# Attention in one-bank steps between the products of a mixture, with TensorE's order written out

## The chip, the cores and the metric

One NeuronCore of a Trainium2 chip runs the whole program. The metric is the device time of one execution in microseconds, the median of several runs. The engines are TensorE (PE in the profile, its weight loads PEld), VectorE (DVE), ScalarE (ACT), GpSimd (POOL) and SyncE (SP, which here only issues transfers).

## What is computed

```
# 4 batches, 8 heads, 576 positions, 64 per head; x is [2304, 512]
scores = q @ k.T / 8;  masked: heads 0-3 the last 32 positions, heads 4-7 every 32nd before
x  = softmax(scores) @ v            # heads side by side
x  = (x @ w_a) * (x @ w_b) @ w_out  # first mixture, 512 -> 1536 -> 512, weights float64
logits = x @ w_gate + log1p(exp(x @ w_noise)) * noise
# the two best of 8 experts per token, weights by softmax over the two
out[token] += weight * relu(x @ w1[e]) @ w2[e]   # 512 -> 1024 -> 512
```

## The kernel before

**Stages.** The first mixture runs in five chunks c of tokens: 512 of each of the four batches, and the four rests of 64 as a fifth of 256. A chunk has twelve steps f of 128 hidden columns. `stage_a` makes `pa` and `pb` (four blocks of 128 of the model width, each three products of a high and a low part, `mm3`, lines 184 to 186), copies `pa` to `a` (line 583), multiplies by `pb` (line 590) and splits the result into `gh` and `gl`. `stage_b` adds the step's share to four outputs `po`, one mixture step later (`prev`). Then eight experts follow.

**Attention.** Batch 0 comes first (`us`), batch 1 beside chunk 0, batches 2 and 3 beside chunks 1 and 2. A `Unit` is a pair of heads; `HPS` orders the four units of a batch, two local and two strided. `T` transposes q and k (line 244), `Q` makes masked scores (274), `E` the softmax (293 to 308; "wide" units with one subtraction, one exponential and one sum, others with an exponential for each block, line 303), `P` transposes the weights (317), copies them (318) and multiplies by v (328). Each is a generator that yields after one or more PSUM banks. Outside batch 0 all of it works in two banks with the tag `t`, which `finish` uses too.

**Queues.** `attq` holds the attention of the next batch, `bgq` the background: `finish` (transposes a chunk's output, line 384, multiplies by the router's weights, 393, and scatters token numbers into a table, `route`), `load_expert` (weights of an expert, lines 141 to 145), `fetch` (gathers tokens of an expert, 639, and transposes them, 648). `point`, three times a mixture step, takes some turns of each queue, so the program's text interleaves them; but the order on each engine is that of a scheduler which estimates times and takes what it thinks ready.

**Weights.** The first mixture's float64 weights come in blocks (`load_m1`), are converted by `split64` (lines 165 to 174, six VectorE and two ScalarE instructions a block) and stand in three units of four steps. The third unit, for f=8 to 11, has no room before batch 1's attention has ended (`drain(); conv_to(30); a1.close()` at f=6 of chunk 0). `late_setup` loads the router's constants and writes the zeros of `out` after the last block.

Of the kernel before, what the change touches and what calls it, by code (L numbers as in the profile page):

```python
# [32 lines left out]
def attention_moe_kernel(ctx: ExitStack, tc: tile.TileContext, q, k, v, w_a, w_b, w_out,  # L33
# [26 lines left out]
    maskS = cpool.tile([72, 4, 72], BF, name="maskS")  # L60
# [10 lines left out]
    with tc.tile_pool(name="setup", bufs=1) as sp:  # L71
# [16 lines left out]
        for i in range(4):  # L88
            nc.vector.tensor_add(maskS[:, i, :], r3f[:, 0], r3f[:, 1])
# [16 lines left out]
    def late_setup():  # L106
        nc.sync.dma_start(wg[:, :, 0:8], w_gate.rearrange("(k p) e -> p k e", p=128))
        nc.sync.dma_start(wg[:, :, 8:16], w_noise.rearrange("(k p) e -> p k e", p=128))
        for b in range(B):
# [11 lines left out]
        zero = rpool.tile([128, DM], F32, name="zero", tag="row", bufs=4)  # L121
        nc.vector.memset(zero, 0.0)
        nr = (NT + PAD) // 128
        nc.sync.dma_start(out.rearrange("(p r) d -> p r d", p=128),
                          zero[:, None, :].to_broadcast([128, nr, DM]))
# [24 lines left out]
    def load_raw(src, m):  # L150

        raw = conv_room["raw"](m)
        last_load[0] = nc.sync.dma_start(raw.rearrange("p (n m) c -> p n (m c)", n=src.shape[1]), src)
        return raw

    last_load = [None]

    def split64(raw, hi, lo):
# [3 lines left out]
        ct = conv_room["ct"](raw.shape[1])  # L162
        m, t = ct[:, 0, :], ct[:, 1, :]
# [3 lines left out]

        nc.vector.tensor_scalar(t, Hw, 0x1FF, None, op0=OP.bitwise_and)
        nc.vector.scalar_tensor_tensor(L.bitcast(F32), L.bitcast(U32), 2.0 ** -32, t, op0=OP.mult, op1=OP.add)
        yield  # L170
        nc.vector.scalar_tensor_tensor(m, Hw, i32(0x80000000), m, op0=OP.bitwise_and, op1=OP.bitwise_or)
        nc.scalar.activation(hi, v(m.bitcast(F32)), AF.Copy)  # L172
        nc.vector.tensor_scalar(Hw, m, i32(0xFF800000), None, op0=OP.bitwise_and)
# [23 lines left out]
    class Unit:  # L197
# [36 lines left out]
        def T(self):  # L234


            n, g = self.n, self.g
            self.qT, self.kT = (self.tile(t, [128, S]) for t in ("qT", "kT"))
            for src, dst, act in ((self.ql, self.qT, True), (self.kl, self.kT, False)):
                dv = dst.rearrange("c (p j) -> c j p", j=6) if self.local else dst.rearrange("c (j p) -> c j p", j=8)  # L240
                for half in range(2):
                    ps = self.bank("T", [128, g, n])
                    for jj in range(g):
                        nc.tensor.transpose(ps[:, jj, :], src[:, g * half + jj, :, :], ident[:n, :n])
                    if act:
                        nc.scalar.activation(dv[:, g * half:g * half + g, :], ps, AF.Copy)
                    else:
                        nc.vector.tensor_copy(dv[:, g * half:g * half + g, :], ps)  # L248
                    yield
# [5 lines left out]
        def Q(self, half):  # L255
            n, g, m = self.n, self.g, self.m
            msk = maskAB[:, half:half + 3, :] if self.local else maskS
            s = self.s[half] = self.tile("s", [n, 2, g, m])
            st = self.tile("sst", [96, 1 if self.wide else 2, 8])
            self.mx, self.sm[half] = st[:n, 0, 0:2 * g], st[:n, 0 if self.wide else 1, 0:2 * g]  # L260
            self.src = []
            for x in range(2):
                ps = self.bank("Q", [n, g, m])
                if self.pemask:
                    nc.tensor.matmul(ps, identb[:n, :n], msk, start=True, stop=False)
                for ii in range(g):
                    hh, jl = self.group(x, ii)
                    i = g * half + jl
                    if self.local:
                        r0, q0, k0 = 64 * hh, 96 * i, 96 * i - 32 if i else 0  # L270
                    else:
# [645 lines left out]
```

## Time and profile before

| | |
|---|---|
| median of 3 runs | 1211.13 us (1207.8 to 1213.44) |
| the profiled execution | 1204.69 us, its span 1202.9 us |
| TensorE busy | 1132.1 us, 94% |
| VectorE, ScalarE, GpSimd busy | 540.9, 404.7, 146.2 us |
| mean granted clock | 0.95 of full speed |

The rows come from the profiled execution, whose own time is 6.4 us under the median. [...] A busy time sums the durations of instructions that may overlap, so it bounds work from above.

### The profile page before, as it was taken

How to read it: one execution, taken by the hardware profiler on the slowest of the kernel's cores; microseconds unless marked ns; L12 is line 12 of the kernel's file. 1: busy time of each engine (PE TensorE's matmuls, PEld its weight loads, DVE VectorE, ACT ScalarE, POOL GpSimd, SP SyncE). 2: the span in 40 equal slices, each digit the busy share in tenths (PEclk: the TensorE clock that was granted, in tenths of full speed). 3: DMA queues.
4: the chain of work that ended last, by engine and by line, in shares of the span. 5: the costliest groups of instructions: out<-in, count | busy, mean ns of one | idle time of the engine just before them, and what ended most of it. 6: DMA issues, size and time to landing. Idle time of an engine off the chain costs nothing.

```text
span 1202.9 us, 16056 instructions
## 1 busy us (share of the span) xinstructions
PE 1132.1 (94%) x6381; PEld 953.0 (79%) x6381; DVE 540.9 (45%) x1154; ACT 404.7 (34%) x866; POOL 146.2 (12%) x136
## 2 busy tenths in 40 slices
PE   6989987899998999989999979999999999999996
PEld 4767765687876778878889869988899998898995
DVE  7899346825256524361313734235433434332111
ACT  4555444422133313241213533235333333232111
POOL 0000000000002000200200122222112222221012
PEclk9979967999996899978999989999999999999998
DMA  7653013590012100030000562337526454433033
GB/s 189 168 170 126 15 29 105 148 335 18 20 50 62 36 20 11 23 108 5 1 1 36 146 151 57 78 79 214 155 79 149 105 125 114 123 93 58 5 40 47
DMA packets 89430, 105.03 MB, mean 87 GB/s; under 512 B 43520, under 2 KB 50304, under 8 KB 89344
## 3 DMA queue, kind: packets, MB, share of 16 engines
q1 hardware_dynamic: 79232, 82.89, 23.6%
q0 software_dynamic: 10112, 21.02, 9.3%
q8 instruction: 52, 0.85, 0.3%
q14 instruction: 34, 0.28, 0.1%
HBM read 78.53 MB, written 25.35 MB: 86 GB/s over the span
## 4 chain that ended last, share of the span: by engine, by line
PE 66%; DMA 8%; DVE 4%; ACT 3%; issue 2%; POOL 1%; SPq 0%; ACTq 0%; DVEq 0%; POOLq 0%
PE ph L184 5%; PE ph L185 5%; PE py L184 5%; PE ph L186 5%; DMA st<-in_moe_w_dram 5%; PE py L185 5%; PE py L186 5%; PE pa L184 3%; PE pa L185 3%; PE pa L186 3%; PE po L184 3%; PE po L185 3%; PE pb L186 3%; PE pb L185 3%; PE pb L184 3%; PE po L186 3%
## 5 line engine op out<-in xcount | busy, mean ns | idle before, releaser
L767 DVE SCALAR_TENSOR_TENSOR hl<-ph,hh 128x256 fp32r<-128x256 f32 (+1 forms) x128 | 62.1, 489 | 195.3 <-ACT hh L766 191.5
L766 ACT ACTIVATE hh<-ph 128x256 fp32r<-128x256 f32 (+1 forms) x128 | 55.1, 434 | 206.4 <-PE ph L186 204.0
L463 POOL DMA_INDIRECT table<-pay,sli x36 | 38.0, 1056 | 669.2 <-DVE sli L450 650.3
L590 DVE TENSOR_TENSOR a<-a,pb 128x512 f32<-128x512 f32 (+1 forms) x60 | 37.9, 631 | 124.9 <-PE pb L186 119.1
L791 POOL DMA_INDIRECT out_dram<-y,tb x40 | 64.7, 1618 | 189.1 <-ACT y L790 126.6
L583 ACT ACTIVATE a<-pa 128x512 f32<-128x512 f32 (+1 forms) x60 | 33.2, 553 | 115.9 <-PE pa L186 109.6
L591 ACT ACTIVATE gh<-a 128x512 fp32r<-128x512 f32 (+1 forms) x60 | 35.2, 587 | 107.0 <-DVE a L590 92.9
L639 POOL DMA_INDIRECT g<-x,tb x40 | 40.9, 1022 | 190.7 <-PE tt L648 161.7
L318 ACT ACTIVATE pT<-tt 128x288 f32<-128x288 f32 (+1 forms) x64 | 25.4, 408 | 73.9 <-PE tt L317 69.0
L592 DVE TENSOR_TENSOR gl<-a,gh 128x512 fp32r<-128x512 f32 (+1 forms) x60 | 38.1, 636 | 23.2 <-ACT gh L591 23.2
L328 PE MATMUL tt<-pT,vl 72*64 72x72 f32 (+1 forms) x448 | 40.0, 306 | 3.2 <-ACT pT L318 2.4
L274 PE MATMUL tt<-kT,qT 64*72 64x72 f32 (+1 forms) x336 | 39.0, 290 | 3.5 <-DVE kT L248 2.0
L274 PEld LDWEIGHTS tt<-kT,qT 64*72 64x72 f32 (+1 forms) x336 | 31.5, 178 | 13.2 <-issue 5.6
L184 PE MATMUL pa<-xh,w6h 128*128 128x512 f32 (+1 forms) x80 | 31.8, 398 | 10.5 <-ACT w6h L172 6.5
L328 PEld LDWEIGHTS tt<-pT,vl 72*64 72x64 f32 (+1 forms) x448 | 28.7, 181 | 16.2 <-ACT pT L318 8.6
L317 PE MATMUL tt<-ident,s 72*72 72x72 f32 (+1 forms) x224 | 34.0, 299 | 4.4 <-DVE s L308 2.1
L184 PE MATMUL pa<-xh,w0h 128*128 128x512 f32 (+1 forms) x80 | 34.7, 434 | 1.9 <-ACT xh L366 1.6
L317 PEld LDWEIGHTS tt<-ident,s 72*72 72x72 f32 (+1 forms) x224 | 26.0, 164 | 13.0 <-issue 4.1
L185 PE MATMUL pa<-xl,w0h 128*128 128x512 f32 (+1 forms) x80 | 33.9, 423 | 2.4 <-DVE xl L367 2.4
L184 PE MATMUL py<-w6h,hh 128*128 128x512 f32 x80 | 31.9, 400 | 4.4 <-ACT y L790 2.5
L184 PE MATMUL py<-w2h,hh 128*128 128x512 f32 x80 | 32.6, 408 | 2.1 <-ACT hh L766 1.3
L186 PE MATMUL pa<-xh,w0l 128*128 128x512 f32 (+1 forms) x80 | 32.4, 405 | 0.0
(292 smaller groups left out, 3296.2 us busy)
## 6 DMA issues: line engine op xcount, KB each, us to landing
st<-in_moe_w_dram SPq DMA_DIRECT2D x64, 512.0 KB
out_dram<-zero SPq DMA_DIRECT2D x1, 6656.0 KB
x<-row SPq DMA_DIRECT2D x16, 256.0 KB
raw<-in_moe_w_a_dram SPq DMA_DIRECT2D x6, 512.0 KB
raw<-in_moe_w_b_dram SPq DMA_DIRECT2D x6, 512.0 KB
raw<-in_moe_w_out_dram SPq DMA_DIRECT2D x6, 512.0 KB
raw<-in_moe_w_a_dram SPq DMA_DIRECT2D x3, 1024.0 KB
raw<-in_moe_w_b_dram SPq DMA_DIRECT2D x3, 1024.0 KB
```

Of the source, the lines that this page charges most:

```text
L184: nc.tensor.matmul(ps, w[0], x[0], start=start, stop=False)
L185: nc.tensor.matmul(ps, w[0], x[1], start=False, stop=False)
L186: nc.tensor.matmul(ps, w[1], x[0], start=False, stop=stop)
L274: nc.tensor.matmul(ps[:, ii, :], self.qT[r0:r0 + 64, q0:q0 + n], self.kT[r0:r0 + 64, k0:k0 + m], start=not self.pemask, stop=not self.pema ...
L317: nc.tensor.transpose(ps[:, ii, :], self.s[half][:, x, ii, :], ident[:n, :n])
L328: nc.tensor.matmul(ps[64 * hh:64 * hh + 64, jl, :], self.vl[:, hh, g * half + jl, :], pT[:, x, ii, :], start=True, stop=True)
L463: ins = nc.gpsimd.indirect_dma_start(out=table, out_offset=bass.IndirectOffsetOnAxis(ap=sli[:, 2 * j + kk:2 * j + kk + 1], axis=0), in_=pa ...
L592: nc.vector.tensor_sub(gl, a, gh.bitcast(F32))
L639: nc.gpsimd.indirect_dma_start(out=g, out_offset=None, in_=x2, in_offset=bass.IndirectOffsetOnAxis(ap=TB[e, t][:, 0:1], axis=0))
L766: nc.scalar.activation(hh, ph, AF.Relu)
L767: nc.vector.scalar_tensor_tensor(hl, ph, 0.0, hh.bitcast(F32), op0=OP.max, op1=OP.subtract)
L791: ins = nc.gpsimd.indirect_dma_start(out=out, out_offset=bass.IndirectOffsetOnAxis(ap=TB[e, t][:, 0:1], axis=0), in_=y, in_offset=None, co ...
```

## The change

Attention's generators become plain functions that each fill one bank (`T(i)`, `Q(half, x)`, `P(half, x)`, `PV(half)`, with `E` called at the end of the second `Q`), and `att_pipe` writes out their order with a yield after each. The loop over mixture steps stands in a block that keeps TensorE's instructions in the order of the program (`manual_schedule`). `point` comes six times a step, every six products, and takes one attention step; `bgq` gets a turn at each third point, in the last chunk at each second. The buffers of the conversion leave the attention pool, so the weights of f=8 and 9 get room right after batch 0, and those of f=10 and 11 take over the conversion's own buffers. Batch 0 uses no wide units. `split64` needs one scratch row of a block in place of two; the strided mask is kept once and broadcast; rows of the chunk's output are held in pairs. The zeros of `out` are written in 13 parts in the background of chunk 3 (`clear_out`), the router's constants loaded at the start of chunk 1.

```diff
+    def clear_out():
+        zero = xpool["g"].tile([128, DM], F32, name="zero", tag="x00h")
         nc.vector.memset(zero, 0.0)
         nr = (NT + PAD) // 128
...
         nc.sync.dma_start(x2[NT:NT + PAD, :].rearrange("(p r) d -> p r d", p=128),
                           zero[:, None, :].to_broadcast([128, PAD // 128, DM]))
+        yield
         for b in range(B):
             nc.sync.dma_start(x2[S * b + CT:S * b + S, :], zero[:TL, :])
+        yield
+        to = out.rearrange("(p r) d -> p r d", p=128)
+        for r in range(0, nr, 2):
+            nc.sync.dma_start(to[:, r:r + 2, :], zero[:, None, :].to_broadcast([128, 2, DM]))
+            yield
...
+            if self.wide and i // 2:
+                nc.vector.tensor_copy(dv[:, g * half:g * half + g, :], ps)
+            else:
+                nc.scalar.activation(dv[:, g * half:g * half + g, :], ps, AF.Copy)
...
+            if x == 1:
+                self.E(half)
...
+    def att_pipe(us, ahead, done=None):
+        for i in range(4):
+            us[0].T(i)
+            yield
+        if ahead < len(us):
+            us[ahead].load_qk()
+        if ahead == 2:
+            us[1].load_v()
+        for n, u in enumerate(us):
+            last = us[n - 1] if n else None
+            nxt = us[n + 1] if n + 1 < len(us) else None
+            for x in range(2):
+                u.Q(0, x)
+                yield
+            if last:
+                for x in range(2):
+                    last.P(1, x)
+                    yield
+            u.Q(1, 0)
+            yield
+            if last:
+                last.PV(1)
+                if done:
+                    done(last)
+                if n + ahead - 1 < len(us):
+                    us[n + ahead - 1].load_v()
+                yield
+            u.Q(1, 1)
+            yield
+            for i in range(2):
+                if nxt:
+                    nxt.T(i)
+                    yield
+            for x in range(2):
+                u.P(0, x)
+                yield
+            for i in range(2, 4):
+                if nxt:
+                    nxt.T(i)
+                    yield
+            if nxt and n + 1 + ahead < len(us):
+                us[n + 1 + ahead].load_qk()
+            u.PV(0)
+            yield
+        for x in range(2):
+            u.P(1, x)
+            yield
+        u.PV(1)
+        if done:
+            done(u)
+        yield
...
+    def last_units(pool, f, tags):
+        three = []
+        for i in range(3):
+            shape = [128, 2, KD, 256] if i < 2 else [128, 2, 2, 512]
+            w = pool.tile(shape, F32R, name=f"w{f}{i}", tag=tags[i])
+            three.append((w[:, 0], w[:, 1]))
+        for i in range(2):
+            W[f + i] = (*three, i)
...
-        for f, n in [(0, 1), (1, 1), (2, 2), (4, 2), (6, 2)] + [(f, 1) for f in range(8, NF)]:
+        for f, n in [(0, 1), (1, 1), (2, 2), (4, 2), (6, 2), (8, 2), (10, 1), (11, 1)]:
...
-    us = [Unit(p1tile, bank0, 0, hp, True, i % 2 == 1) for i, hp in enumerate(HPS)]
+    us = [Unit(p1tile, bank0, 0, hp, True, False) for hp in HPS]
...
+    a1.close()
+    tp = m1.enter_context(tc.tile_pool(name="third", bufs=1, reuse_waits="tile"))
+    att = ExitStack()
+    apool = att.enter_context(tc.tile_pool(name="att", bufs=1, side="right", reuse_waits="tile"))
+    last_units(tp, 8, ("w80", "w81", "w82"))
+    def atile(name, shape):
+        if name in ("ql", "kl"):
+            return stage.tile(shape, F32, name=name, tag=f"st{int(name == 'kl')}")
+        return apool.tile(shape, F32, name=name, tag=name, bufs=2 if name in ("s", "sst") else 1)
+    def attend(b, wide):
+        us = [Unit(atile, bank1, b, hp, False, wide) for hp in HPS]
+        us[0].load_qk()
+        us[0].load_v()
+        return att_pipe(us, 1)
+    attq.append(attend(1, False))
...
+        def half(tag, w):
+            ps = psum.tile([128, n], F32, name="pa" if tag == "A" else "pb", tag=tag)
+            for i, kd in enumerate(HPS):
+                mm3(ps, tuple(t[:, kd, cols] for t in w), xT[c, kd], i == 0, i == KD - 1)
+                if i == 1:
+                    point()
+            return ps
+        pa = half("A", wa)
...
+            if 2 * (j + 1) in (J, 2 * J):
+                point()
...
+    with tc.manual_schedule(engines={mybir.EngineType.PE}):
+        prev = None
+        npt = [0]
+        for c, f in ORDER:
+            n0, n1 = nconv[0], min(48, 12 + 4 * (f + 1) if f < 6 else 36 + 6 * (f - 5))
+            def point():
+                npt[0] += 1
+                if c == 0:
+                    conv_to(n0 + (n1 - n0) * ((npt[0] - 1) % 6 + 1) // 6)
                 advance(attq)
...
+                if npt[0] % (2 if c == NCH - 1 else 3) == 0:
+                    advance(bgq)
+            if c == 0 and f == 6:
+                conv_to(36)
+                last_units(cp, 10, ("u0", "u1", "u2"))
+                conv_room["raw"] = lambda m: rpool.tile([128, 512, 2], I32, name="raw", tag=f"row{next_of(2)}")
+                conv_room["ct"] = lambda m: rpool.tile([128, 512], I32, name="ct", tag="x2T")
+            if f == NF - 1:
+                while attq:
+                    advance(attq)
+                if c == 0:
+                    conv_to(48)
+            if c == 1 and f == 0:
+                late_setup()
+            if (c, f) == (B - 1, 0):
+                bgq.append(clear_out())
+                att.close()
+                xr = ctx.enter_context(tc.tile_pool(name="xr", bufs=1, side="right"))
+                xpool[0, 0] = xr
+                xpool["g"] = xr
+            if (c, f) == (B - 1, 2):
+                for kd in HPS:
+                    xf[B, kd] = mpool.tile([128, TL * B], F32, name="xf", tag="xf", bufs=4)
+                    nc.sync.dma_start(xf[B, kd], tails[:, kd, :])
+            if 0 < c < B - 1 and f == 0:
+                attq.append(attend(c + 1, True))
+            if (c, f) == (NCH - 1, 5):
+                bgq.append(load_expert(0))
+            if (c, f) == (NCH - 1, 8):
+                bgq.append(fetch(0, [0, 1, 2]))
+            g = stage_a(c, f, point)
+            if f == NF - 1 and c + 1 < NCH:
+                for kd in HPS:
+                    split_kd(c + 1, kd)
+            if prev is not None:
+                rows = stage_b(*prev, point)
+                if rows is not None:
+                    bgq.append(finish(prev[0], rows))
+            prev = (c, f, g)
+        drain()
+        last_rows = stage_b(*prev, pump)
```

## Rows read from the trace of the kernel before

**Rows 1.** The page, part 1: busy time, share of the span, instructions.

```profile
PE 1132.1 (94%) x6381; PEld 953.0 (79%) x6381; DVE 540.9 (45%) x1154; ACT 404.7 (34%) x866; POOL 146.2 (12%) x136
```

**Rows 2.** Stage view: stretch, length, PE, PEld, DVE, ACT, POOL busy (instructions), clock, transfers, GB/s.

```profile
0.00:81.80 81.80, 66.63 (x387) 49.76 (x388) 70.28 (x160) 44.16 (x111) 2.57 (x20) 0.92 0.67 175
81.80:147.30 65.50, 65.28 (x342) 50.58 (x342) 48.04 (x76) 32.79 (x90) 0.00 (x0) 1.00 0.26 82
147.30:197.50 50.20, 41.65 (x267) 31.47 (x266) 23.32 (x49) 23.41 (x84) 0.00 (x0) 0.66 0.17 46
197.50:242.80 45.30, 37.39 (x147) 27.73 (x146) 37.04 (x70) 18.55 (x32) 0.00 (x0) 0.96 0.54 162
242.80:346.50 103.70, 103.70 (x535) 83.85 (x535) 35.26 (x64) 23.84 (x42) 0.00 (x0) 1.00 0.33 103
346.50:398.10 51.60, 45.27 (x314) 34.99 (x313) 33.93 (x89) 20.81 (x40) 8.57 (x8) 0.71 0.28 69
398.10:505.50 107.40, 107.40 (x602) 86.31 (x602) 45.66 (x108) 28.36 (x49) 8.42 (x8) 1.00 0.08 20
505.50:543.00 37.50, 34.43 (x235) 27.31 (x234) 21.66 (x41) 13.94 (x28) 0.26 (x1) 0.81 0.30 92
543.00:643.60 100.60, 100.60 (x461) 82.78 (x461) 24.31 (x73) 20.17 (x35) 8.01 (x8) 0.97 0.01 1
643.60:715.40 71.80, 61.85 (x432) 56.40 (x430) 36.60 (x105) 31.59 (x65) 11.72 (x11) 0.95 0.43 115
715.40:1202.90 487.50, 467.92 (x2673) 421.81 (x2673) 164.74 (x322) 147.07 (x295) 106.62 (x81) 0.99 0.40 97
```

**Rows 3.** TensorE's instructions in order, chunk 1: start, duration, engine, line, operands, count.

```profile
251.68 0.39 PE L184 MATMUL pa<-xh,w0h 128*128 128x512 f32 x1
...
259.35 0.39 PE L184 MATMUL pa<-xh,w0h 128*128 128x512 f32 x1
```

**Rows 4.** TensorE's instructions in order, pause after chunk 1; in brackets the wait before.

```profile
389.50 0.60 PE L328 MATMUL tt<-pT,vl 72*64 72x72 f32 x12 [0.44 <-ACT pT L318]
391.31 0.67 PE L317 MATMUL tt<-ident,s 72*72 72x72 f32 x8 [1.21 <-DVE s L308]
```

**Rows 5.** TensorE's groups by line, 398.1 to 505.5: operands, count, busy us, mean ns, idle.

```profile
L274 PE MATMUL tt<-kT,qT 64*96 64x128 f32 (+1 forms) x68 | 6.5, 260 | 0.0
...
L393 PE MATMUL tt<-wg,x2T 128*128 128x16 f32 x32 | 4.1, 259 | 0.0
...
L317 PE MATMUL tt<-ident,s 72*72 72x72 f32 (+1 forms) x28 | 3.0, 235 | 0.0
L328 PE MATMUL tt<-pT,vl 128*64 128x96 f32 (+1 forms) x40 | 2.5, 247 | 0.0
L384 PE MATMUL tt<-ident,row 128*128 128x128 f32 x16 | 2.4, 272 | 0.0
L244 PE MATMUL tt<-ident,ql 72*128 72x72 f32 (+1 forms) x14 | 1.8, 245 | 0.0
```

**Rows 6.** The page, part 5: costliest groups of the whole span.

```profile
L318 ACT ACTIVATE pT<-tt 128x288 f32<-128x288 f32 (+1 forms) x64 | 25.4, 408 | 73.9 <-PE tt L317 69.0
...
L274 PE MATMUL tt<-kT,qT 64*72 64x72 f32 (+1 forms) x336 | 39.0, 290 | 3.5 <-DVE kT L248 2.0
```

**Rows 7.** ScalarE's groups by line and shape, 0 to 245.

```profile
L303 ACT ACTIVATE s<-s,sst 72x72 f32<-72x72 f32 x32 | 10.8, 342 | 0.7 <-DVE sst L301 0.7
...
L303 ACT ACTIVATION_READ_ACCUMULATOR s<-s,sst 72x1 f32 x32 | 6.0, 188 | 0.0
```

**Rows 8.** TensorE's instructions in order, beside batch 0's attention.

```profile
41.80 0.63 PE L186 MATMUL pa<-xh,w0l 128*128 128x512 f32 x1
42.23 0.63 PE L185 MATMUL pb<-xl,w1h 128*128 128x512 f32 x1
```

**Rows 9.** GpSimd's instructions in order: the first gather.

```profile
706.23 0.99 POOL L639 DMA_INDIRECT g<-x,tb  x1 [10.05 <-PE pb L186]
```

More of the change, by code (lines that the diff above doesn't have):

```diff
@@ new lines, in Q @@
+            msk = maskAB[:, half:half + 3, :] if self.local else maskS[:, None, :].to_broadcast([72, 4, 72])
+            if x == 0:
+                self.s[half] = self.tile("s", [n, 2, g, m])
+                st = self.tile("sst", [96, 1 if self.wide else 2, 8])
+                self.mx, self.sm[half] = st[:n, 0, 0:2 * g], st[:n, 0 if self.wide else 1, 0:2 * g]
+                self.src = []
+            s = self.s[half]
+            ps = self.bank("Q", [n, g, m])
+            if self.pemask:
+                nc.tensor.matmul(ps, identb[:n, :n], msk, start=True, stop=False)
@@ new lines, in Q @@
+            for ii in range(g):
+                hh, jl = self.group(x, ii)
+                i = g * half + jl
+                if self.local:
+                    r0, q0, k0 = 64 * hh, 96 * i, 96 * i - 32 if i else 0
+                else:
+                    r0, q0 = 64 * (i % 2), 72 * (4 * hh + i // 2)
+                    k0 = q0
+                nc.tensor.matmul(ps[:, ii, :], self.qT[r0:r0 + 64, q0:q0 + n], self.kT[r0:r0 + 64, k0:k0 + m],
+                                 start=not self.pemask, stop=not self.pemask or ii == g - 1)
@@ L506, in attention_moe_kernel @@
     ORDER = [(c, f) for c in range(NCH) for f in range(NF)]
-    WA, WB, WO = [None] * 3, [None] * 3, [None] * 3
+    W = {}
     for u in range(2):
-        WA[u], WB[u], WO[u] = (unit_pair(3 * u + i) for i in range(3))
+        three = [unit_pair(3 * u + i) for i in range(3)]
+        for f in range(4 * u, 4 * u + 4):
+            W[f] = (*three, f % 4)
+    def last_units(pool, f, tags):
[6 more added lines that the diff above has]
+            W[f + i] = (*three, i)
+    NPAIR = 18
     def load_m1():
@@ new lines, in load_m1 @@
+        raws = []
+        for k, (_, f, n, i) in enumerate(blocks):
+            while len(raws) < min(k + 2, len(blocks), 99 if k >= NPAIR else NPAIR):
+                raws.append(load_raw(blocks[len(raws)][0], 512 * blocks[len(raws)][2]))
+            at = W[f][3]
+            yield from split64(raws[k], *(t[:, :, 128 * at:128 * (at + n)] if i < 2 else t[:, at:at + n, :]
+                                          for t in W[f][i]))
+    cp = m1.enter_context(tc.tile_pool(name="conv", bufs=1))
@@ L539, in attention_moe_kernel @@
+    conv_room["ct"] = ct_tile
     conv = load_m1()
@@ L584, in stage_a @@
         point()
-        pb = psum.tile([128, n], F32, name="pb", tag="B")
-        for kd in HPS:
-            mm3(pb, tuple(t[:, kd, w[1]:w[1] + 128] for t in WB[w[0]]), xT[c, kd], kd == HPS[0], kd == HPS[-1])
+        pb = half("B", wb)
         gh = mpool.tile([128, n], F32R, name="gh", tag="gh", bufs=2)
```

254 lines of the change are left out of this document (62 added, 192 removed).

## The prediction

> **What bounds the kernel now.** I read the page first: TensorE is busy 94% of the span, every other engine under half [rows 1]. That share hides the question, because a transposition at half clock counts as busy like a product at full clock; so I cut the span at the copies `a<-pa` of line 583, one per mixture step, and read the stages [rows 2]. The bounds are the copies of f=0 of each chunk (81.8, 242.8, 398.1, 543.0, 643.6), the last copy before a pause and the first after it (147.3 and 197.5; 346.5 for f=11 of chunk 1; 505.5 for f=11 of chunk 2), and the first product of the experts (715.4).
>
> The reader is to see two kinds of stretch. In 242.8 to 346.5 and 398.1 to 505.5 TensorE is never idle, at granted clock 1.00. In 147.3 to 197.5, 346.5 to 398.1 and 505.5 to 543.0 hardly a mixture step ends: attention, left over, runs nearly alone, at a mean clock of 0.66, 0.71 and 0.81, with short idle spells. The waits there are of TensorE for what attention itself has just asked of VectorE and ScalarE (0.44 us for a copy of line 318, 1.21 us for the scaled scores of line 308) [rows 4]: chains of one head pair with no other work between. So before 543 us the kernel is bound by TensorE where mixture and attention mix, and by attention's chain and the lower clock where they don't.
>
> **The cost of dense work.** Between two like products of consecutive mixture steps stand 33 products in 7.67 us, so one 512-column product takes 0.2324 us [rows 3]. A step is 36 of them (24 for `pa` and `pb`, 12 for `po`), 8.37 us, a chunk 100.4 us. From the copy of f=0 to that of f=11 lie 11 steps, 92.0 us; in chunk 2 they took 107.4 us [rows 2], so 15.4 us paid for what attention and `finish` had in there. By lines that was 68 of the score products, 28 of the transpositions of line 317, 40 products of line 328, 28 transpositions of q and k (14 of each), and the whole `finish` of one chunk (16 transpositions, 32 router products) [rows 5]. A batch shows 112 score products (336 over three batches [rows 6]; the code writes 56, so each shows as two), by the code also 112 of line 328 and 56 transpositions of either kind: about half a batch was there. If `finish` took 5 us of the 15.4 (its rows are busy 6.5 us, overlapping), half a batch took 10.4 and a batch some 21; if `finish` cost nothing, 31. The new order cuts attention into 56 groups a batch where that stretch had it in larger ones, so I take 27 us.
>
> **The change, part by part.** *Order of the mixture.* TensorE now takes its instructions in the order of the program, and the program offers an attention step at six points of each mixture step, every six products, 1.39 us apart. 72 points a chunk for 56 steps: all of a batch is issued by f=9, none is left for a pause. Chunk 1 becomes 100.4 + 27 + 6 (`finish`) = 133 us against 155.3 now; chunk 2 also 133 against 144.9: -22 and -12.
>
> *Chunk 0.* Now 161.0 us, in which the pause also holds back the third weight unit: its room comes free only when attention of batch 1 is done, and 197.5 to 242.8 then runs step by step behind the conversions. The change gives that room right after batch 0's attention. The floor is 100.4 + 27. VectorE was busy 108.4 us in these 161.0 and ScalarE 74.8 [rows 2], so both fit, VectorE at some 80%. Here batch 1's softmax is still eight (six) exponentials one by one, 0.34 us and 0.19 us for the sum each [rows 7]: about 4 us in which the copies of line 318 and others queue on ScalarE. I add 8 us for that and for the first load of batch 1, which waits for a buffer of batch 0: 135 us, -26. Its bounds: 127, nothing exposed, and 161, the conversions as late as now.
>
> *Batch 0's attention.* No products of chunk 0 need run between it any more, units 1 and 3 move their subtraction and sum from VectorE to ScalarE, and kT is copied by ScalarE. [...] TensorE is busy 66.6 of 81.8 us there, VectorE 70.3, ScalarE 44.2 [rows 2]. Fewer products and less VectorE work pull down, the longer softmax chain pulls up. I take 0; bounds -10 and +8.
>
> *One bank per step, two banks `t`.* A step may reuse a bank two points later, some 3 us after it filled it. The copies that empty it take about 0.41 us [rows 6]; the cover is the 12 products between. Where that cover is short, after a `finish` step that takes the other bank, a copy queued behind a longer instruction can still be late; the 6 us for `finish` hold that. Deeper dependences are further apart: five steps or more from the scores to their transposition, some 9 us.
>
> *Mask in one copy, `split64` with a half-size scratch, paired rows, conversion blocks of two units:* the same operations on the same amounts, off TensorE; 0, at most 1 us.
>
> *Chunk 3.* No attention there: 100.6 us now. But part of its f=0 was run ahead, in the pause before; the new order can't. With `finish` it is 100.4 + 6 less what was done by 543; I take 103, +2. The zeros written to `out` move here from the start of chunk 1, where TensorE was never idle beside them; 0.
>
> *Chunk 4 and the start of the experts.* 71.8 us now, of which 61.9 TensorE was busy [rows 2]; the first gather goes out at 706.2 [rows 9]. A chunk of 256 tokens has half-length `pa` and `pb` products and half as many `po`: 50.2 us at full clock, with `finish` 56. Against that stands a detail of the queues: `clear_out` (15 steps) and `finish` (16) share the 24 turns of chunk 3, so seven steps spill over and `finish` of chunk 3 gets to its scatters only at f=7 of chunk 4, with the experts' weights already taking turns. The transpositions of gathered rows are in TensorE's order too, so it stands still if a gather is late. I take 68, -4; bounds 58 and 90.
>
> **Sum.** -26 - 22 - 12 + 2 - 4 = -62. The profiled execution took 1204.7 us (span 1202.9, 1.8 around it), so 1143 on its scale; the median of the runs is 1211.1, 6.4 us more, so 1149. The experts, 487.5 us, keep their code.
>
> **Rivals.** *Chunk 0 doesn't shrink:* conversions, exponentials and copies share two in-order engines, and TensorE, in order, waits for whatever they put late. For it: from 197.5 to 242.8, where only conversions hold the steps up, VectorE is busy 37.0 of 45.3 us. Against: from 81.8 to 147.3 it converted beside attention (48.0 of 65.5 us) and TensorE was busy 65.3 [rows 2]. Time 1149 + 26 = 1175. Chance 0.09.
>
> *The tail takes it back:* the late scatters cost chunk 4 some 20 us instead of giving 4. 1149 + 20, about 1170. Chance 0.06.
>
> *Waits in order, slower than before:* the scheduler's order let TensorE run mixture products while attention waited; the written one doesn't. 168 attention steps and 48 of `finish` stand in it; if each waits 0.29 us the 62 are gone, with 0.5 us, about the shorter of the two waits shown, the time is 1149 + 108 = 1257. For it: those waits exist [rows 4]. Against: they arise where the next step follows at once, and here 1.39 us of products stand between. Chance 0.06, of which 0.05 ends slower. [...]
>
> *The clock falls in the mixed stretches:* many small groups with short gaps. [...] Against: attention stood between products in the dense stretches and the granted clock was 1.00 [rows 2]. Chance 0.03. [...]
>
> *The order isn't the cause:* the pauses are set by loads and remain, no change, 1211. The waits in them are for VectorE and ScalarE, not DMA; chance 0.02.
>
> **How the numbers follow.** The forecast, chance 0.74, is 1149, rounded to 1150; the bounds of its terms are -8 and +15 (chunk 0 from 127 to 150), -18 and +12 (three batches at 21 or 31), -10 and +8 (batch 0), -10 and +22 (the tail). Taken as independent (root of the sum of squares) they give -24 and +30, 1125 to 1179 for the forecast alone. The range runs from 1115, the two largest low bounds and a little of the others, to 1188, which holds the first two rivals. A change of under 0.5%, about 6 us, can't be told from none. Faster: 0.74 + 0.09 + 0.06 + 0.03 = 0.92. Same: 0.02 and 0.01 of the waits, 0.03. Slower 0.05.
>
> **What would show it.** Copies `a<-pa` at an even pace of some 11 us through chunks 0 to 2 and none more than 15 us apart; granted clock 1.00 from f=1 of chunk 0 to the end of chunk 3; no stretch of attention alone; the experts beginning 60 us earlier, and 487 us long as now. Wrong would be: TensorE idle before lines 274 and 317 at every step (order), gaps named `w..h` in chunk 0 (conversions), or the first gather as far behind f=0 of chunk 4 as now, 63 us, or more (tail).

## The result, and the profile after

The changed kernel took 1170.3 us in the median of four runs (1169.4 to 1178.9), the kernel before on the same chip 1212.0 (1207.8 to 1213.4): a ratio of 0.968, 95% interval 0.963 to 0.973. Forecast were 1150. The profiled execution took 1169.4 us with a span of 1167.6; against the 1204.7 of the one before, 35.3 us went, where the sum said 62.

The stage view of the changed kernel, cut as in [rows 2] at the copies `a<-pa` (now line 666) of f=0 of each chunk and at the first product of the experts:

```profile
0.00:87.46 87.46, 61.27 (x369) 44.70 (x370) 63.21 (x141) 53.00 (x180) 2.28 (x19) 0.90 0.61 160
87.46:223.46 136.00, 131.08 (x760) 100.97 (x758) 99.29 (x166) 76.88 (x208) 0.26 (x1) 0.98 0.35 103
223.46:360.77 137.31, 136.59 (x834) 106.93 (x832) 67.46 (x149) 43.78 (x77) 7.93 (x8) 1.00 0.14 37
360.77:496.98 136.21, 136.21 (x828) 106.74 (x827) 67.91 (x150) 43.09 (x76) 7.74 (x8) 1.00 0.30 97
496.98:600.62 103.64, 103.64 (x482) 85.41 (x481) 25.48 (x69) 21.95 (x37) 0.00 (x0) 1.00 0.09 29
600.62:676.60 75.98, 62.59 (x449) 56.51 (x447) 34.47 (x108) 30.00 (x62) 19.04 (x19) 0.96 0.44 108
676.60:1167.60 491.00, 471.41 (x2674) 425.98 (x2672) 167.48 (x327) 149.29 (x300) 106.71 (x81) 0.98 0.40 97
```

| stretch | before | after | difference | forecast |
|---|---|---|---|---|
| to f=0 of chunk 0 (batch 0's attention) | 81.8 | 87.5 | +5.7 | 0 |
| chunk 0 | 161.0 | 136.0 | -25.0 | -26 |
| chunk 1 | 155.3 | 137.3 | -18.0 | -22 |
| chunk 2 | 144.9 | 136.2 | -8.7 | -12 |
| chunk 3 | 100.6 | 103.6 | +3.0 | +2 |
| chunk 4 to the first expert product | 71.8 | 76.0 | +4.2 | -4 |
| experts | 487.5 | 491.0 | +3.5 | 0 |

The pauses are gone: in chunks 1 and 2 the copies stand 8.2 to 13.4 us apart, TensorE idles 0.7 us in the two together, and the granted clock (TensorE's, as a share of full speed) is 1.00, where the last steps of these chunks had been stretches of attention at 0.71 and 0.81 [rows 2]. Three of the prediction's signs were missed: in chunk 0 one copy stands 17.4 us behind the one before (f=1 to f=2, with a wait of 4.1 us for batch 1's scaled scores), over the 15 allowed; the clock is 0.98 there; and the experts begin 38.8 us earlier, not 60. What the sum lacked is shown by three places.

First, the passage between mixture and attention. TensorE's instructions in order, chunk 2 (start, duration, operands):

```profile
382.77 0.39 PE L187 MATMUL pa<-xl,w0h 128*128 128x512 f32 x1
383.00 0.39 PE L188 MATMUL pa<-xh,w0l 128*128 128x512 f32 x1
383.24 0.41 PE L247 MATMUL tt<-ident,kl 72*128 72x72 f32 x4
383.45 0.48 PE L186 MATMUL pa<-xh,w0h 128*128 128x512 f32 x1
383.77 0.39 PE L187 MATMUL pa<-xl,w0h 128*128 128x512 f32 x1
```

Products follow each other in 0.23 us, as in [rows 3]; the one behind a group of attention holds the next up for 0.32 (383.45 to 383.77). So it is behind all 54 groups that stand between products in chunk 2 (0.31 to 0.34, from start to start). That is 0.09 us a group, 5 us for 56 groups. The product ahead of a group of score products or of line 331 is held up as well, 0.32 to 0.33 in all 24 cases, which is another 2 us.

Second, the waits of TensorE until 88 us (line waited for: total, times, longest):

```profile
PE tt L331 <- ACT pT L319: 5.6, 5, 2.2
...
PE tt L247 <- DMA ql<-in_q_dram: 3.8, 1, 3.8
PE tt L318 <- DVE s L310: 3.7, 2, 3.3
PE tt L318 <- ACT xf L334: 3.2, 2, 3.0
```

In the stage of before the like of the first and the last two came to 0.7 us. Batch 0's last products, before and after (the second line is of the changed kernel):

```profile
75.69 1.55 PE L328 MATMUL tt<-pT,vl 72*64 72x72 f32 x16
78.98 1.28 PE L331 MATMUL tt<-pT,vl 72*64 72x72 f32 x16 [0.44 <-ACT pT L319]
```

They began 3.3 us later; behind them stand the 3.8 us for batch 1's first load, ahead of the copy that ends this stage. ScalarE's groups by line up to 82 us show why batch 0 takes longer: 56 exponentials and 56 sums, 29.6 us, where there were 24 of each and four wide ones.

```profile
L306 ACT ACTIVATE s<-sc,sst 72x72 f32<-72x72 f32 (+1 forms) x56 | 18.0, 339 | 3.7 <-PE tt L331 3.6 <-DVE sst L304 0.2
L306 ACT ACTIVATION_READ_ACCUMULATOR s<-sc,sst 72x1 f32 (+1 forms) x56 | 11.6, 208 | 0.0
```

Third, the tail. SP's issues and GpSimd's and TensorE's instructions in order; the gather of the third fence answers to [rows 9]:

```profile
620.20 31.45 SPq L146 DMA_DIRECT2D st<-in_moe_w_dram  x10
655.58 0.34 SPq L716 DMA_DIRECT2D tb<-table  x1
```

```profile
669.95 1.12 PE L731 MATMUL tt<-ident,g 128*128 128x128 f32 x4 [7.41 <-DMA g<-x,tb]
```

```profile
659.46 1.28 POOL L496 DMA_INDIRECT table<-pay,sli  x1 [9.67 <-issue]
661.04 0.97 POOL L496 DMA_INDIRECT table<-pay,sli  x1 [0.30 <-DMA st<-in_moe_w_dram]
662.31 0.98 POOL L722 DMA_INDIRECT g<-x,tb  x1 [0.30 <-issue]
```

The 31.45 us run from the first to the last of ten issues that took 0.37 to 0.38 us each. These weight loads come ahead of the first table on SP, and four of the eight scatters of chunk 3's router, the last at 664.9, behind it, beside the gathers. The first gather goes out 61.7 us behind the copy of f=0 of chunk 4, about the 63 that I named as the sign of trouble in the tail, and TensorE, which has the transposition of gathered rows in its order, stands 7.4 us ahead of `po` products that were ready.

### The profile page after: what moved, and what is told of

It is laid out like the page before. It is cut to its first block, busy times and chain, and to the rows that moved or that the text cites. A ratio compares the mean times of both kernels' runs of the same rounds, so it can differ in the third digit from the quotient of the medians.

```text
span 1167.6 us, 16084 instructions
## 1 busy us (share of the span) xinstructions
PE 1102.8 (94%) x6381; PEld 927.2 (79%) x6381; DVE 525.3 (45%) x1109; ACT 418.0 (36%) x936; POOL 144.0 (12%) x136
## 4 chain that ended last, share of the span: by engine, by line
PE 78%; DMA 10%; DVE 7%; issue 2%; POOL 2%; ACT 1%; SPq 1%; DVEq 0%; ACTq 0%; POOLq 0%
PE ph L186 6%; PE ph L187 6%; PE ph L188 6%; PE py L186 6%; PE py L187 6%; PE py L188 5%; PE po L186 4%; PE pb L186 4%; PE pa L186 4%; PE pb L188 4%; PE pb L187 4%; PE po L188 4%; PE po L187 4%; PE pa L187 4%; PE pa L188 4%; DMA st<-in_moe_w_dram 3%
## 5 line engine op out<-in xcount | busy, mean ns | idle before, releaser
L672 ACT ACTIVATE gh<-a 128x512 fp32r<-128x512 f32 (+1 forms) x60 | 35.3, 588 | 81.2 <-DVE a L671 80.2
L277 PEld LDWEIGHTS tt<-kT,qT 64*72 64x72 f32 (+1 forms) x336 | 30.4, 149 | 18.2 <-issue 14.9
L318 PE MATMUL tt<-ident,s 72*72 72x72 f32 (+1 forms) x224 | 30.9, 263 | 11.9 <-DVE s L310 7.8
L277 PE MATMUL tt<-kT,qT 64*72 64x72 f32 (+1 forms) x336 | 39.1, 253 | 0.7 <-DVE s L286 0.7
L331 PEld LDWEIGHTS tt<-pT,vl 72*64 72x64 f32 (+1 forms) x448 | 22.3, 156 | 18.6 <-issue 8.6
L331 PE MATMUL tt<-pT,vl 72*64 72x72 f32 (+1 forms) x448 | 29.8, 270 | 5.6 <-ACT pT L319 5.6
L731 PE MATMUL tt<-ident,g 128*128 128x128 f32 x160 | 26.0, 281 | 9.5 <-DMA g<-x,tb 8.1
L731 PEld LDWEIGHTS tt<-ident,g 128*128 128x128 f32 x160 | 20.6, 145 | 15.1 <-DMA g<-x,tb 7.6
L187 PE MATMUL py<-w6l,hh 128*128 128x512 f32 x80 | 32.6, 407 | 0.0
## 6 DMA issues: line engine op xcount, KB each, us to landing
ql<-in_q_dram SPq DMA_DIRECT2D x16, 144.0 KB
```

Source lines behind the costliest of these rows:

```text
L187: nc.tensor.matmul(ps, w[0], x[1], start=False, stop=False)
L277: nc.tensor.matmul(ps[:, ii, :], self.qT[r0:r0 + 64, q0:q0 + n], self.kT[r0:r0 + 64, k0:k0 + m], start=not self.pemask, stop=not self.pema ...
L318: nc.tensor.transpose(ps[:, ii, :], self.s[half][:, x, ii, :], ident[:n, :n])
L331: nc.tensor.matmul(ps[64 * hh:64 * hh + 64, jl, :], self.vl[:, hh, g * half + jl, :], self.pT[:, x, ii, :], start=True, stop=True)
L731: nc.tensor.transpose(ps[:, kd, :], g[:, 128 * kd:128 * kd + 128], ident)
```

## The experiments

Times of whole kernels are medians; stages are read from one profiled execution each. "Before" ran on the same chip each time with medians of 1207 to 1210. The expert stage has the same instructions in all kernels and took 482.6 to 491.0 us in their profiled executions; so differences of a few us are read from the stages ahead of it and not from the totals. Stages have a spread too: up to f=0 of chunk 0 the eight kernels that keep the changed one's batch 0 and its loads took 84.5 to 88.1 us, and the seven that keep its tail took 75.2 to 80.2 us from f=0 of chunk 4 to the first expert product.

**The order without the rest, and the rest without the order.** The first kernel is the changed one with the block around the mixture's loop taken out:

```diff
-    with tc.manual_schedule(engines={mybir.EngineType.PE}):
+    if True:
```

> The changed kernel without the block that fixes TensorE's order: attention's one-bank steps, the earlier weight rooms and all else are kept, and TensorE's instructions are again placed by the scheduler. Theory (the order is the cause): attention is again left over at the ends of chunks 0 to 2, stretches without a mixture step come back, and the time returns to between 1190 and 1215 us. Rival (the small steps and the early rooms are what helps): no such stretch, within 10 us of the changed kernel's 1170.

Measured: 1191.4, ratio 0.984 (0.978 to 0.991). ScalarE's copies `a<-pa` in order, the two around the end of chunk 1, and the stage between them (columns as above):

```profile
338.32 0.60 ACT L666 ACTIVATE a<-pa 128x512 f32<-128x512 f32 x1 [1.25 <-PE pa L188]
...
373.54 0.60 ACT L666 ACTIVATE a<-pa 128x512 f32<-128x512 f32 x1 [2.06 <-PE pa L188]
```

```profile
334.00:373.54 39.54, 32.85 (x251) 25.74 (x250) 20.76 (x43) 14.60 (x29) 8.08 (x8) 0.86 0.28 76
```

The pause is back: 35.2 us without a mixture step, TensorE busy 32.9 of 39.5. Chunks 0 to 2 end with such steps of 39.1, 35.2 and 40.1 us, where before they had one each of 50.2, 51.6 and 37.5. So the theory's sign is there, but not its whole price: of some 40 us, 21 hang on the order (1191.4 less 1170.3), the other 19 came without it, by shorter pauses in chunks 0 and 1 (142.2 and 144.0 us); which of the change's other parts gave them, no run shows.

The second kernel is the one before with only its loop put into such a block (the same line, added there).

> The kernel before, with nothing changed but that its first mixture stands in the block that fixes TensorE's order: attention's steps as before, several of them at each of three points of a mixture step, the third weight unit's room free as late as before. Theory (the order takes the pauses away by itself, but with several groups behind one point it pays waits for banks and for copies, and chunk 0 keeps its late room): no step more than 20 us long in chunks 1 and 2, which take 140 to 150 us each, chunk 0 155 to 165; 1190 to 1205 in all. Rival 1 (the order alone gives the whole gain): 1165 to 1175. Rival 2 (in order, without the small steps, the waits outweigh the pauses): over 1216.

Measured: 1203.7, ratio 0.995 (0.992 to 0.998). Chunk 0 took 152.5, chunk 1 166.0, chunk 2 144.8. SP's issues and TensorE's first step of batch 2, in order:

```profile
222.04 11.58 SPq L126 DMA_DIRECT2D x<-zero  x1
233.66 9.01 SPq L129 DMA_DIRECT2D x<-zero  x4
242.77 3.22 SPq L216 DMA_DIRECT2D ql<-in_q_dram  x2
```

```profile
251.37 1.19 PE L244 MATMUL tt<-ident,ql 96*128 96x96 f32 x6 [20.98 <-DMA ql<-in_q_dram]
```

The pauses are gone, but one step of 36.7 us stands at the start of chunk 1: the issues on zeros hold SP for 20.6 us, batch 2's first load is behind them, and the mixture behind the step that needs it. My expectation of 140 to 150 for chunk 1 missed that; without the 21 us it would have held. Order alone gives 0.5%, the rest alone 1.6%, both 3.2%: the order needs loads that come early enough for it.

**The zeros.** In the changed kernel they were written in one go again at the start of chunk 1:

```diff
 def late_setup():
     ...
+        zero = rpool.tile([128, 2, DM], F32, name="zero", tag="row1")[:, 0]
+        nc.vector.memset(zero, 0.0)
+        nc.sync.dma_start(out.rearrange("(p r) d -> p r d", p=128), ...)
+        nc.sync.dma_start(x2[NT:NT + PAD, :].rearrange("(p r) d -> p r d", p=128), ...)
+        for b in range(B):
+            nc.sync.dma_start(x2[S * b + CT:S * b + S, :], zero[:TL, :])
     ...
-                bgq.append(clear_out())
```

> The changed kernel with the zeros of the output and of the padding rows written in one go at the start of chunk 1, as before, instead of in 15 turns of chunk 3. Theory (SP's queue works in order and its issues stall behind those zeros, so batch 2's first load comes some 20 us late, and in the written order the mixture stands behind the transposition that needs it; with the order alone one such wait took 21.0 us): one step of chunk 1 takes over 28 us, chunk 1 18 to 24 us longer, chunk 3 unchanged, and from the copy of f=0 of chunk 4 to the first expert product 4 to 8 us less than 76.0, since the router gets its turns; 1178 to 1190 in all. Rival (the zeros are hidden wherever they stand, as I priced them): chunk 1 within 2 us, 1160 to 1167.

Measured: 1183.7, ratio 0.980 (0.975 to 0.985). SP's issues, then TensorE's step that needs the load:

```profile
185.84 0.64 SPq L123 DMA_DIRECT2D out_dram<-zero  x1
186.53 11.04 SPq L125 DMA_DIRECT2D x<-zero  x1
197.61 5.66 SPq L128 DMA_DIRECT2D x<-zero  x1
...
204.76 1.23 SPq L242 DMA_DIRECT2D vl<-in_v_dram  x1
```

```profile
213.68 1.23 PE L340 MATMUL tt<-pT,vl 72*64 72x72 f32 x16 [17.70 <-DMA vl<-in_v_dram]
```

The price was right, the place wrong. SP's queue is still placed by the scheduler, which put the zeros ahead of batch 1's last load of v, so one step late in chunk 0 took 31.2 us; the copy of f=0 of chunk 1 came at 244.7 instead of 223.5, chunk 1 took 137.8. The tail went from 76.0 to 69.5, as expected of the turns that became free. So the zeros were no cost only because they moved: left where they were they cost 21 us up to f=0 of chunk 1, and 13 in all. In the kernel before they held SP as long (21.4 us, from 235.4 to 256.8); SP's issues and TensorE's first step of batch 2 there:

```profile
236.12 10.87 SPq L126 DMA_DIRECT2D x<-zero  x1
...
256.92 3.23 SPq L216 DMA_DIRECT2D ql<-in_q_dram  x2
```

```profile
266.35 0.66 PE L244 MATMUL tt<-ident,ql 96*128 96x96 f32 x6
```

That step came 23.5 us into chunk 1, and TensorE ran on with products until then without a pause [rows 2]. In the changed kernel the issues of the zeros stand at the end of chunk 2:

```profile
473.43 0.59 SPq L125 DMA_DIRECT2D x<-zero  x1
...
479.07 17.86 SPq L133 DMA_DIRECT2D out_dram<-zero  x13
```

They still fill 23.5 us of SP, so cutting them into parts didn't make them shorter; they cost nothing because TensorE waits for no load there (it is never idle in chunks 2 and 3).

**How attention is cut.** Two steps at every second point, and six at one point of a mixture step:

```diff
-                advance(attq)
+                if npt[0] % 2 == 0:
+                    advance(attq)
+                    advance(attq)
```

> Attention advances two steps at every second point (behind 12 products) instead of one at every point (behind 6). Theory (what my 27 us for a batch missed is the passage between mixture and a small group: 432 mixture products beside attention took 107 us where they take 100 alone, some 0.12 us for each of 56 groups): half as many passages, chunks 0 to 2 each 3 to 4 us shorter, about 1160 in all. Rival 1 (the cost lies in the groups' own instructions): chunks unchanged within 1 us. Rival 2 (the second group of a pair waits for a bank): some 0.3 us for each of 28 pairs, each chunk 5 to 8 us longer.

Measured: 1166.7, ratio 0.964 (0.958 to 0.969). Chunks 1 and 2 of the pairs:

```profile
224.84:360.41 135.57, 133.71 (x833) 107.48 (x832) 66.65 (x149) 41.70 (x77) 7.94 (x8) 1.00 0.14 37
360.41:495.99 135.58, 133.72 (x831) 107.54 (x830) 67.13 (x150) 41.72 (x78) 7.73 (x8) 1.00 0.30 97
```

TensorE is busy 2.9 and 2.5 us less than in the changed kernel, 0.09 to 0.10 us for each of the 28 passages that the code saves. (In chunk 1's rows the groups between products fall from 56 to 33, since some steps stand beside one of `finish`; that is 0.13 us for each, as the product ahead of some groups gains too.) Waits rise from 0.7 and 0 to 1.9 us a chunk, so 1.7 and 0.6 are left, less than the 3 to 4 expected. Chunk 0 grew by 4.3 and the stage ahead of it shrank by 3.0, since the wait for batch 1's first load is no longer ahead of the copy. The theory holds in part. The second rival doesn't: in each chunk three of the four waits listed, 1.2 of 1.7 us, are at line 417, where a step of `finish` follows a pair, and not at the second group of a pair.

```diff
-                advance(attq)
+                if npt[0] % 6 == 0:
+                    for _ in range(6):
+                        advance(attq)
```

> Attention advances six steps at one point of each mixture step (behind 36 products), so four groups of a block follow the one that used their bank of t with one group between. Theory (the 1.39 us of products between two groups are the cover for the copies that empty a bank, 0.41 us and the signals about it): 37 groups of a batch wait about 0.5 us each, less the passages saved (some 6 us), so chunks 0 to 2 become 10 to 15 us longer each and the kernel takes 1200 to 1215. Rival (no cover is needed): each chunk 5 to 6 us shorter, about 1152.

Measured: 1222.8, ratio 1.010 (1.005 to 1.015), 1% slower than before. Chunk 1 of it:

```profile
246.60:398.78 152.18, 142.64 (x833) 114.52 (x832) 67.32 (x149) 42.55 (x78) 7.96 (x8) 0.94 0.12 33
```

Chunks 1 and 2 grew by 14.9 and 16.5, chunk 0 by 25.9. TensorE idles 9.5 us in chunk 1, half of the 18 I had put on bank waits (1.7 of them for a load of v and 1.0 for scaled scores, the rest almost all for instructions that empty a bank). The rest goes with the clock, 0.94 in the mean: the busy time is 6.1 us above the changed kernel's, though 46 passages fewer should have saved some 4. So the products between the steps are the cover, and where they stand decides over 52 us.

**The tail.** More turns for the background queue from chunk 3 on, then two empty turns ahead of the router's rank products as well:

```diff
-                if npt[0] % (2 if c == NCH - 1 else 3) == 0:
+                if npt[0] % (2 if c >= B - 1 else 3) == 0:
```

> From chunk 3 on the background queue gets every second point instead of every third (as it already does in chunk 4), 36 turns in chunk 3 instead of 24, so the zeros and the router of chunk 2 end within chunk 3 and the router of chunk 3 starts with f=0 of chunk 4. Theory (the tail lost because the router's last scatters of chunk 3, and behind them the first table and gathers, come late): TensorE no longer stands 7.4 us for the gathered rows, and from the copy of f=0 of chunk 4 to the first expert product it takes 66 to 71 us instead of 76.0; chunk 3 unchanged within 1 us. Rival (the table's load is late for another reason, the loads of the expert's weights ahead of it on the same queue): 74 to 77 us.

Measured: 1163.3, ratio 0.961 (0.956 to 0.966); from the copy of f=0 of chunk 4 to the first expert product 70.4 us, chunk 3 104.1. The theory holds: the wait for the gathered rows is gone. But another stands in its place, in TensorE's order:

```profile
635.81 0.19 PE L470 MATMUL tt<-ms,tri 128*128 128x8 bf16 x1 [6.80 <-DVE ms L465]
```

The rank products now come before the router's chain on VectorE and ScalarE has ended. So:

```diff
-        yield
+        for _ in range(3):
+            yield
         rk = pt([128, J + 1, 8])
```

> The kernel with more turns for the background queue (every second point from chunk 3 on) and two empty turns ahead of the router's rank products. Theory (with the turns alone TensorE stood 6.8 us at those products for the router's chain on VectorE and ScalarE, which the written order brought too close): this wait gone, from the copy of f=0 of chunk 4 to the first expert product 63 to 67 us instead of 70.4. Rival (the gathered rows then come too late, and TensorE waits there): 69 to 73.

Measured: 1162.2, ratio 0.962 (0.957 to 0.966); the tail 67.7, a little over the 63 to 67 expected, since 2.8 us of that wait are left. With the spread of the experts the total can't be told from that of the kernel with the turns alone. The stage is 2.7 us shorter, less than the spread of kernels with the same tail; that the empty turns did it rests on the wait, 6.8 us there and 2.8 here.

**Batch 0 and batch 1's first load.** Four kernels. Batch 0's work divided as before, with all copies of k on VectorE:

```diff
-            if self.wide and i // 2:
+            if i // 2:
...
-    us = [Unit(p1tile, bank0, 0, hp, True, False) for hp in HPS]
+    us = [Unit(p1tile, bank0, 0, hp, True, i % 2 == 1) for i, hp in enumerate(HPS)]
```

> The changed kernel with batch 0's work divided as before: units 1 and 3 subtract and sum on VectorE with one exponential each half, and all copies of k transposed go to VectorE (batch 1's too). Theory (batch 0 grew because its softmax and copies on ScalarE became longer, 56 exponentials with 29.6 us there against 24 with 13.6, and TensorE waits 12.5 us for the copies and scaled scores of lines 318 and 331 where it waited 0.7): the copy of f=0 of chunk 0 comes at 81 to 84 us instead of 87.5. Rival (what lacks there is the mixture products that the scheduler could put between): 86 to 89.

Measured: 1162.9, ratio 0.961 (0.957 to 0.965). The copy of f=0 came at 83.3, and batch 0's last products began at 72.5 instead of 79.0, so ScalarE's work was the cause of batch 0's growth (which part of it, the softmax or the copies of k, this run doesn't tell). A wait of 5.9 us for batch 1's first load stands behind them. Chunk 0 took 138.7, 2.7 more. The second of the two lines alone:

> The changed kernel with one edit: units 1 and 3 of batch 0 wide again (their subtraction, sum and copy of k transposed on VectorE), k of units 0 and 2 still copied by ScalarE. It parts what the version with five edits gave up to the copy of f=0 of chunk 0 (74.2 us instead of 87.5). Theory (ScalarE's longer softmax held batch 0's end back by some 9 us, and once it is gone the first load of batch 1, with its buffer freed by batch 0's last step, is exposed in full): batch 0's last product at 69 to 71 us, then a wait of 4 to 7 us for that load, the copy at 78 to 81. Rival 1 (the copies of k on VectorE made no difference, so this is the earlier version of batch 0 again): 82.5 to 84. Rival 2 (the dealing of the buffers gives nothing, as when it was tried alone): 74 to 75.

Measured: 1168.3, ratio 0.968 (0.966 to 0.970). TensorE's last products of batch 0, its first step of batch 1, and that unit's transposition of scaled scores:

```profile
69.50 1.56 PE L331 MATMUL tt<-pT,vl 72*64 72x72 f32 x16
77.19 0.71 PE L247 MATMUL tt<-ident,ql 96*128 96x96 f32 x3 [6.12 <-DMA ql<-in_q_dram]
...
105.76 0.71 PE L318 MATMUL tt<-ident,s 96*128 96x96 f32 x3 [6.16 <-DVE s L310]
```

The theory, in all its numbers: batch 0 ends 9.5 us earlier, the load is then exposed for 6.1, the copy at 80.5. Yet chunk 0 took 141.8 and the copy of f=0 of chunk 1 came at 222.4, 1.1 us earlier than in the changed kernel: TensorE next stands for batch 1's softmax, whose scaling (line 310) is placed among VectorE's conversions.

The load alone, dealt to buffers that are free earlier, and batch 1's first step put off by four points:

```diff
-    nslot = [0]
+    nslot = [2]
```

> The changed kernel with batch 0's loads dealt to their six buffers from another starting place, so that the two buffers which batch 1's first load takes over are free before batch 0's last step instead of after it. Theory (the first step of batch 1 waits 3.8 us for a load that waits for that buffer): this wait gone, the copy of f=0 of chunk 1 at 218.5 to 220.5 us instead of 223.5. Rival (as in the late first step: what is late is the softmax of batch 1's first unit behind the conversions, and its wait grows by what the load gives back): 222 to 224.5.

Measured: 1172.2, ratio 0.970 (0.965 to 0.974). The wait for the load is gone, and the copy of f=0 of chunk 1 comes at 224.9, just beyond the rival's 224.5.

```diff
-                advance(attq)
+                if npt[0] > 4:
+                    advance(attq)
```

> The changed kernel with batch 1's first attention step four points later, behind the first mixture step of chunk 0 instead of inside its first product group. Theory (the first step waits 3.8 us for its load, whose buffer batch 0 frees late, and the mixture stands behind it in TensorE's order): stage 0 and chunk 0 together 3 to 5 us shorter, 218 to 220 us up to the copy of f=0 of chunk 1. Rival (the wait only moves, the second head pair's load is as late): 222 to 224.

Measured: 1171.0, ratio 0.967 (0.963 to 0.972); the copy of f=0 of chunk 1 at 228.4, beyond the rival. Putting the step off only makes the softmax later, with a wait of 5.3 us.

**Five edits together** (the turns, three empty turns, the wide units, the dealing of the buffers, and pairs of steps from chunk 1 on):

> The changed kernel with five edits together: a turn of the background queue at every second point from chunk 3 on, three empty turns ahead of the rank products, units 1 and 3 of batch 0 wide again, batch 0's loads dealt so that batch 1's first is early, and from chunk 1 on two attention steps at every second point. If the gains add: the copy of f=0 of chunk 1 at 216 to 219 us, chunks 1 and 2 135 to 136 us each, chunk 3 104, chunk 4 to the first expert product 64 to 68, the experts 486 to 491 as in the other runs, 1143 to 1153 in all. Rival (they share a cause, the conversions' pace in chunk 0, or the tail's chain): 1156 to 1163, no better than the best of the single edits.

Measured: 1143.1 (six runs, 1138.6 to 1146.4), ratio 0.944 (0.941 to 0.948), better than either kernel. The stages but the experts (the 1.00 in the first row is not to be taken as a reading: in the changed kernel the view gives 1.00 up to 70 us too, where products of `pa` begin 0.42 us apart, 62.82 and 63.24, much as in [rows 8]):

```profile
0.00:74.23 74.23, 62.28 (x369) 45.45 (x370) 58.92 (x141) 41.02 (x112) 2.28 (x19) 1.00 0.63 160
74.23:211.85 137.62, 131.21 (x756) 100.79 (x755) 109.82 (x178) 80.11 (x210) 0.26 (x1) 0.98 0.39 117
211.85:347.31 135.46, 133.60 (x833) 107.58 (x832) 66.28 (x149) 41.85 (x78) 8.25 (x8) 1.00 0.14 37
347.31:482.76 135.45, 133.59 (x831) 107.60 (x830) 66.78 (x150) 41.83 (x78) 8.26 (x8) 1.00 0.31 97
482.76:586.85 104.09, 104.09 (x496) 85.70 (x495) 25.92 (x77) 21.72 (x37) 7.73 (x8) 1.00 0.09 29
586.85:654.94 68.09, 61.45 (x435) 55.97 (x433) 33.90 (x100) 29.66 (x61) 12.17 (x11) 0.97 0.44 121
```

The copy of f=0 of chunk 1 came at 211.9, 11.6 us earlier than in the changed kernel, where the wide units alone gave 1.1 and the dealing alone lost 1.4, both no more than the spread of the three kernels with the same code up to there (223.5 to 225.0): two waits in a row, each of which hid the other. The other three edits change TensorE's order from chunk 1 on only. Chunk 0 gave back only 1.6 here and 5.8 with the wide units alone; what VectorE does differently there I did not part, and it stays open.

## Why the prediction was right, and where it was off

**The mechanism held.** Attention left over was what the pauses were made of, the written order with a step at each point leaves none, and each chunk from 0 to 2 became shorter by most of what was forecast (-51.7 of -60). Without the order the pauses came back.

**Batch 0's attention: 0 taken, +5.7 measured.** I set fewer products and less VectorE work against a longer softmax chain and let them cancel. They don't: the chain through ScalarE sets this stage, and work taken from TensorE and VectorE there frees nothing: with the wide units back batch 0 ends 9.5 us earlier. Of the 5.7, though, only 3.3 are batch 0's end. The wait of 3.8 us for batch 1's first load also falls into this stage, and I had put it into chunk 0. The bound of +8 held.

**A batch at 27 us: about 30 to 31 measured.** Chunks 1 and 2 less 100.4 and my 6 for `finish` leave 30.9 and 29.8. (`finish` itself is nearer 5: chunk 3 of the kernel with more turns, which holds all of one, took 104.1, and its products some 99.0, since the last `pa` in it is chunk 4's and half as long.) The step that was off is the reckoning from the stretch of chunk 2 [rows 5]. I took 92.0 us of it for 11 steps, 396 products. TensorE's rows of `pa`, `pb` and `po` in that stretch, with their counts (columns as in [rows 2], TensorE alone):

```profile
398.10:505.50 107.40, 34.03 (x132) 1.00 0.08 20
398.10:505.50 107.40, 32.53 (x124) 1.00 0.08 20
398.10:505.50 107.40, 30.69 (x120) 1.00 0.08 20
```

That is 376, for the scheduler had run some ahead and left others for later; at 0.2324 us they take 87.4 us, so attention and `finish` had 20.0 us and not 15.4. By the same reckoning, 5 us for `finish` and twice the rest, a batch took 30 there already. My raise from 21 to 27 for the smaller groups was no less than the 5 to 7 us that all passages of a batch cost; what was too small is the 21.

**Chunk 0: -26 taken, -25.0 measured.** The match is in part luck. TensorE idles 4.9 us in it, and with the 3.8 for the first load, which fell ahead of it, this is about the 8 that I had added. The dearer batch is mostly made up for, since its stretch holds 421 mixture products and not 432: there is no `po` of a chunk before.

**Chunk 4 and the start: -4 taken, +4.2 measured.** I saw that seven steps spill over and that TensorE would stand if a gather is late, and still priced it as a gain. It is the rival of the tail, at 8 us instead of its 24. The turns give it back (70.4), the empty turns a little more (67.7).

**The experts: +3.5.** Nothing of the change: the same code took from 482.6 to 491.0.

**The zeros: 0, for a wrong reason.** I took them as hidden wherever they stand because TensorE was never idle beside them before. That was so because the scheduler let mixture products run until the load had come; in the written order they cost 21 us where they were.

**Waits in order.** Few: 5.6 us of idle TensorE between 88 and 600 us, not the 62 that this rival needed. With six steps at a point it comes true (1222.8), at my point of decision: the cover.

**The clock.** 1.00 from chunk 1 to chunk 3, with small groups passing through two banks all the time and TensorE idle for 0.7 us in all; so this trace doesn't test what many short gaps would do. In the blocks of six, where TensorE idled 9.5 us of 152 in chunk 1, the clock was 0.94, and in the pauses of before, with short idle spells, 0.66 to 0.81 [rows 2]; no run parts the idle spells from the rest there. Nor does a run show what time this rival would have given: its 0.03 among the faster outcomes was my estimate.

## What to carry to other kernels

An order written by hand takes away the slack that let an engine run ahead, so before writing one look for what that slack hid: here a queue of SP that zeros held for 20.6 us (with the order alone), and a chain through ScalarE, which held batch 0's end back by 9.5 us. Price the passage between two kinds of work, not only the work: one product after a small group tells it (0.32 us here to the next, where it is 0.23 between products). And try edits that shorten one chain together: alone each of two gave nothing clear of the spread, because the next wait took its place, and together they gave 11.6 us.

## What the runs showed of the hardware that was not expected

One issue of SP on zeros took 10.9 to 11.6 us (in the kernel before, with the order alone, and with the zeros early), where the issue of a block of the experts' weights took 0.37 in the median, and everything behind it on that queue waited. It is the issue of the 2048 KB for the padding rows. It stands right behind the one transfer of 6656 KB to `out`, whose own issue took 0.64 (in the kernel before and with the zeros early). In the changed kernel, with no such transfer ahead of it, the issue of the same 2048 KB took 0.59. So the 2048 KB themselves don't make the issue long: it was long in the three kernels with the 6656 KB ahead of it and short in the one without. Whether size or shape of that transfer does it, no run shows. With the zeros early, the 11.04 us and the 5.66 of the issue behind it stood ahead of batch 1's last load of v, for which TensorE then waited 17.7 us.
